# Weight sums split wholly on VectorE, their writes issued ahead of a step's loads, divisors sooner, key maxima one step later

## The chip, the cores and the metric

The kernel runs on one core of one Trainium2 chip. The metric is the device time of one execution in microseconds (us), as the median of several runs. TensorE (PE) multiplies matrices, VectorE (DVE), ScalarE (ACT) and GpSimd (POOL) do elementwise work, and SyncE (SP) issues every DMA of this kernel. Each engine works through its own list of instructions in order. Where an instruction waits, everything behind it on that engine waits too.

## The reference, cut to what matters

An attention over batch 4, heads 8, sequence 768, head dimension 64 is followed by a feed-forward part with 3072 tokens, 512 model columns and 2048 hidden columns:

```
k_sum = k.reshape(B, H, nb, block, D).max(axis=3)      # maxima of 32 keys
v_sum = v.reshape(B, H, nb, block, D).mean(axis=3)     # means of 32 values
scores_l = scale * q k^T, masked to |i - j| < 16;  scores_s = scale * q k_sum^T + log(block)
a = softmax of both side by side
attn_out = a @ [v, v_sum]
h = x @ w_in                      # x: attn_out as (3072, 512)
g = h * tanh(softplus(h))
out = g @ w_out
```

## The kernel before

**Tiles and steps.** The tokens are cut into 12 chunks of 256 and 6 groups of 512 (two chunks). The hidden columns are cut into 16 blocks of 128. A step is one (group, block): `ph` multiplies the group's x by a block of w_in (L501), `ff_act` applies the activation (L508), `ff_split` splits the result into a rounded upper part `ah` (ACT, L517) and the rest `al` (DVE, L519), and `ff_out` multiplies both by the block of w_out into `po` (L529). `ff_out` of step i-2 runs in step i. Groups 0 and 1 (steps 0 to 31) compute `ph` directly. From step 32 on, steps go in pairs: `ff_in_pair` computes the `ph` of two blocks with seven products of quarter blocks instead of eight (L738), as a Strassen-like scheme, and DVE puts them together (L748 to L756, tile `change`).

**Weight sums.** That scheme needs sums and differences of quarter blocks of w_in. They are made once, for eight pairs p of blocks, in two halves per pair: `first_sums` (L705, L706) and `second_sums` (L711, L712). `split_sums` rounds each into an upper part (L696, on ACT) and a rest (L697, on DVE). All of it lies in one scratch tile, `area` (in the profile: `results`). The halves are made in steps 19 to 30, one per step, and in steps 34, 36, 38 and 40. `keep` queues their writes to DRAM (`w_sums`, L689) in a list, `send` issues that list in the next step, and `load_sums` (L723) later reads a pair's sums into one of two buffers. A half overwrites the area that the half before is being written from, so its first DVE instructions wait until those writes have landed.

**Attention units.** One unit is one chunk and one pair of heads, 48 in all. From unit 18 on, units go two by two, at the steps in `begins`: 19, 22, 25, 29, 33, 37 and so on, every fourth step to 73. For a pair of units that begins at step i: `scores` (L345) with the maxima (L366) and exponents (L377, ACT) in step i, divisors (`rs`, L392 and L393, DVE) and normalisation (L397, POOL) in step i for the first unit and step i+1 for the second, transposes (`pt_ps`, L403, PE) in step i+2, values (`x_ps`, L429) where the next pair begins. `x_sum` (L457 to L463, DVE) turns the values into the x of a later group.

**Loads of a step.** `loads` issues, in this order: the queries and keys `qk` of the next two units (L304), what `keys` holds, the values `vw` (L321, L322), and what `sums` holds. `keys` of a unit copies its key maxima `km` into the `qk` tile (POOL, L309). For the first unit of a batch's head pair it first reduces the keys to `km` (DVE, L273) and then loads the values for their means, `vsum` (L239). `sums` of such a unit makes the means `vq` (DVE, L294, L295), writes them to a tile `vm` (L300) and loads the next head pair's keys `ks` (L235). `ks` and `vsum` share one buffer, so the four units of a batch form a chain: ks, km, vsum, vq, ks, km, and so on. Two such chains fall into the part that the change touches: units 24 to 27 (used by the scores of steps 29 and 33) and units 36 to 39 (scores of steps 53 and 57).

**What sets the order.** Up to step 18 the order is written out by hand and the diff does not touch it. From step 19 on it comes from two loops. A whole step (19 to 31) and the second step of a pair run `norms(i)`, `loads(i)`, `send()`, then queued x sums, `ff_out`, `turns`, and `weight_sums(i)` at the end. Between the first products of a pair and the next ones, `between` runs the exponents of a second unit. The steps at which a unit's `keys` and `sums` come are set by `put`:

```
put("keys", i + 2 * j, u + 2)
put("sums", min(i + 2 * j + 1, later - 1), u + 2)
```

Here j is 0 for the first and 1 for the second unit, and `later` is the step at which the next pair begins.

Of the kernel before, what the change touches and what calls it, by code (L numbers as in the profile page):

```python
# [10 lines left out]
F32R = mybir.dt.float32r  # L11
# [55 lines left out]
def fused_kernel(ctx: ExitStack, tc: tile.TileContext, q0, qk, kt, v0, vw, vs, w_in, w_out, out):  # L67
    nc = tc.nc
# [168 lines left out]
    def load_value_source(b, hp):  # L237
        vsum = sources[b, hp, 1] = stage.tile([VP, BLK, BLK], F32, tag="sum", name=f"vsum{b}_{hp}", bufs=1)
        nc.sync.dma_start(vsum, vs[b, hp].rearrange("p (d j) -> p d j", j=BLK))  # L239
# [71 lines left out]
    def att_load_keys(c, hp):  # L311
        b, th = divmod(c, CPB)
        if th == 0:
            key_summary(b, hp)
            load_value_source(b, hp)
        att_key_summary(c, hp)
# [8 lines left out]
    def att_summaries(u):  # L325

        for i, fs in ((u, (value_means, value_summary)), (u + 1, (load_key_source,))):
            if i < len(todo) and todo[i][0] % CPB == 0:
                for f in fs:
                    f(todo[i][0] // CPB, todo[i][1])  # L330
# [40 lines left out]
    def att_exponents(c, hp):  # L371

        u = units[c, hp]
        pr, nm = u["p"], u.pop("m")
        sm = small.tile([P, NQ], F32, tag="sm", name=f"sm{c}_{hp}")
        for s in range(NQ):
            nc.scalar.activation(pr[:, s, :], pr[:, s, :], AF.Exp, scale=-1.0, bias=nm[:, s:s + 1],  # L377
                                 accum_out=sm[:, s:s + 1])
        u["sm"] = sm
# [164 lines left out]
    steps = [(g, fc) for g in range(NG) for fc in range(NFC)]  # L544
# [135 lines left out]
    def send():  # L680
        while unsent:
            unsent.pop(0)()
# [10 lines left out]
            keep(p, part, 0, t[:, CH:3 * CH])  # L693

    def split_sums(p, first, whole, upper):
        nc.scalar.copy(upper.bitcast(F32R), whole)  # L696
        nc.vector.tensor_sub(whole.bitcast(F32R), whole, upper)  # L697
        keep(p, 0, first, upper)
        keep(p, 1, first, whole)
# [25 lines left out]
    def ff_in_pair(g, fc, pair, between):  # L725

        w = buffer(pair)
        banks = []

        def products(*found):  # L730
            ps = ps_w.tile([P, TG], F32, tag="w", name=f"ph{g}_{fc}_{len(banks)}")
            banks.append(ps)
            for half, m in enumerate(found):
                wh, wl = (w[:, part, (4, 3, 1, 2, 5, 6, 7).index(m), :] for part in range(2))
                xh, xl = x_piece(g, m)
                for a in range(2):
                    for n, (w_, x) in enumerate(((wh, xh), (wh, xl), (wl, xh))):
                        nc.tensor.matmul(turned(ps[:, half * CH:(half + 1) * CH]), w_[:, a * P:(a + 1) * P],  # L738
                                         turned(x[:, a, :]), start=(a == 0 and n == 0), stop=(a == 1 and n == 2))
            return ps  # L740

        first_, second = (ff.tile([P, TG], F32, tag="t", name=f"h{g}_{fc + k}", bufs=2) for k in range(2))
        low, high = slice(0, CH), slice(CH, TG)
        nc.scalar.copy(second, products(1, 3))
        between()
        ps = products(2, 6)
        nc.scalar.copy(first_[:, low], ps[:, low])  # L747
        nc.vector.tensor_sub(change, second[:, high], ps[:, low])  # L748
        nc.vector.tensor_add(change, second[:, low], change)
        nc.vector.tensor_add(first_[:, high], ps[:, high], change)  # L750
        ps = products(7, 5)
        nc.vector.tensor_add(second, ps, second)
        nc.vector.tensor_sub(second[:, low], second[:, low], ps[:, high])
        ps = products(4)
        nc.vector.tensor_add(first_[:, low], ps[:, low], first_[:, low])  # L755
        nc.vector.tensor_add(second[:, low], ps[:, low], second[:, low])  # L756
        st[g, fc], st[g, fc + 1] = first_, second

    at = {}

    def put(what, i, *found):
        at.setdefault((what, i), []).extend(found)
# [4 lines left out]
    for k, i in enumerate(begins):  # L767
        pair = [2 * n + 2 + 2 * k, 2 * n + 3 + 2 * k]
        later = begins[k + 1] if k + 1 < len(begins) else i + 4
        put("scores", i, *pair)  # L770
        put("turns", i + 2, *pair)
        put("values", later, *pair)
        for j, u in enumerate(pair):
            put("norms", i + j, u)
            put("keys", i + 2 * j, u + 2)
            put("sums", min(i + 2 * j + 1, later - 1), u + 2)

    def found(what, i):
        return [todo[u] for u in at.get((what, i), ()) if u < len(todo)]
# [1 line left out]
    def loads(i):  # L781
        for u in at.get(("scores", i), ()):
            if u + 2 < len(todo):
                att_queries(*todo[u + 2])
        for unit_ in found("keys", i):
            att_load_keys(*unit_)
        for u in at.get(("values", i), ()):
            if u + 2 < len(todo):
                att_load_values(*todo[u + 2])
        for u in at.get(("sums", i), ()):  # L790
            att_summaries(u)

    def norms(i):
        for unit_ in found("norms", i):
            att_divisors(*unit_)
            att_normalize(*unit_)
# [34 lines left out]
    for i in range(done, whole_steps):  # L831
        ff_in(*steps[i])
        ff_act(*steps[i])
        values(i)
        some = scores(i)
        lower = ff_split(*steps[i])
        for unit_ in some:
            att_exponents(*unit_)
        lower()
        norms(i)  # L840
        loads(i)
        send()
        for _ in waiting[:2 if some else 1]:
            waiting.pop(0)()
        ff_out(*steps[i - 2])
        turns(i)
        if whole_steps - i in (3, 2):
            load_sums(3 - (whole_steps - i))
        weight_sums(i)

    late_exponents = []
    for i in range(whole_steps, len(steps), 2):
        pair = (i - whole_steps) // 2
        ff_in_pair(*steps[i], pair, lambda: [att_exponents(*late_exponents.pop()) for _ in late_exponents[:]])
        ff_act(*steps[i])
        ff_act(*steps[i + 1])
        norms(i)
        ff_split(*steps[i])()
        while waiting:
            waiting.pop(0)()  # L860
        loads(i)
        send()
        ff_out(*steps[i - 2])
        weight_sums(i)
        load_sums(pair + 2)
        values(i + 1)
        some = scores(i + 1)
        if some:
            att_exponents(*some[0])
            late_exponents.extend(some[1:])  # L870
        ff_split(*steps[i + 1])()
        norms(i + 1)
        loads(i + 1)
        send()
        for _ in waiting[:2]:
            waiting.pop(0)()
        ff_out(*steps[i - 1])
        turns(i + 1)
        weight_sums(i + 1)
# [46 lines left out]
```

## Time and profile before

| | |
|---|---|
| median of 3 runs | 671.72 us (671.13 to 673.95) |
| the profiled execution | 673.55 us, of which the span in the trace is 671.6 us |
| PE busy in the span | 613.0 us (91%) |
| weight loads of PE (PEld) | 528.5 us (79%) |
| DVE | 427.8 us (64%) |
| ACT | 350.9 us (52%) |
| POOL | 82.5 us (12%) |
| DMA | 141.77 MB, mean 211 GB/s |

In the profile's picture of the span in 40 slices, PE is at 9 tenths or more almost everywhere. The exceptions are the beginning, one slice at 48% of the span, and slices 12 to 18 (about 185 to 302 us), where it falls to between 5 and 9 tenths. In the same slices the granted clock of TensorE falls below its full level. Lower down, the page lists groups of instructions and what ended the idle time before them. A wait is worth something only if PE waits for it in the end.

### The profile page before, as it was taken

What the parts mean: (1) busy time and instruction counts of PE and PEld (TensorE: products, weight loads), DVE (VectorE), ACT (ScalarE), POOL (GpSimd) and SP (SyncE); (2) the same over time, 40 slices, a digit from 0 to 9 for tenths busy, and PEclk for the clock granted to TensorE, in tenths of its full rate; (3) what the DMA queues carried; (4) which work ended last, traced back from release to release, by engine and by line L of the source; (5) the groups of instructions that cost most, each with busy time, mean ns of one, the idle gap of its engine ahead of it and who ended that gap; (6) DMA issues with size and microseconds to landing.
All of it is one profiled execution on the core that took longest, in us unless ns stands there. A gap on an engine that the chain in (4) does not pass through costs nothing.

```text
span 671.6 us, 12969 instructions
## 1 busy us (share of the span) xinstructions
PE 613.0 (91%) x4848; PEld 528.5 (79%) x4848; DVE 427.8 (64%) x1078; ACT 350.9 (52%) x827; POOL 82.5 (12%) x119
## 2 busy tenths in 40 slices
PE   4899999999979756479999999889999999999997
PEld 4787777788868545368889898778898988998996
DVE  5999999954655345366776676657675564744433
ACT  4985758764635224145656654535664654333232
POOL 4522122000120000001001101011100100000000
PEclk9999999999999787769999999999999999999999
DMA  9977766514475226659987867658867745365421
GB/s 281 284 231 257 256 210 225 201 47 136 147 236 185 96 71 198 246 180 338 331 302 242 271 231 255 237 190 311 288 210 243 251 147 213 128 264 197 141 101 63
DMA packets 50222, 141.77 MB, mean 211 GB/s; under 512 B 8816, under 2 KB 15728, under 8 KB 50160
## 3 DMA queue, kind: packets, MB, share of 16 engines
q1 hardware_dynamic: 50160, 140.94, 62.1%
q8 instruction: 39, 0.64, 0.4%
q14 instruction: 23, 0.19, 0.1%
HBM read 117.83 MB, written 20.97 MB: 207 GB/s over the span
## 4 chain that ended last, share of the span: by engine, by line
PE 54%; DMA 13%; DVE 12%; ACT 5%; SPq 3%; issue 2%; POOL 0%; DVEq 0%; POOLq 0%; ACTq 0%
PE po L529 25%; PE ph L738 18%; PE ph L501 5%; DMA vsum<-vs 3%; DMA w_sums<-results 3%; DMA qk<-qk 3%; PE x_ps L429 2%; PE sc L345 2%; DVE al L519 2%; DMA w_early_in<-w_sums 2%; DMA ks<-kt 2%; PE pt_ps L403 1%; DVE vq L294 1%; SPq L689 1%; DVE km L273 1%
## 5 line engine op out<-in xcount | busy, mean ns | idle before, releaser
L397 POOL TENSOR_TENSOR pr<-pr,rs 128x480 f32<-128x480 f32 x48 | 59.3, 1236 | 380.7 <-DVE rs L393 229.4
L738 PE MATMUL ph<-xh,w_early_in 128*128 128x256 f32 x512 | 100.1, 280 | 5.8 <-ACT a L508 5.8
L529 PE MATMUL po<-w_early_out_hi,al 128*128 128x512 f32 x240 | 93.5, 389 | 1.1 <-DVE al L519 1.1
L529 PE MATMUL po<-w_early_out_hi,ah 128*128 128x512 f32 x240 | 94.4, 393 | 0.0
L529 PE MATMUL po<-w_early_out_lo,ah 128*128 128x512 f32 x240 | 93.3, 389 | 0.0
L738 PEld LDWEIGHTS ph<-xh,w_early_in 128*128 128x128 f32 x512 | 83.7, 192 | 6.1 <-ACT a L508 6.1
L508 ACT ACTIVATE h<-h 128x512 f32<-128x512 f32 x64 | 36.9, 623 | 91.9 <-DVE h L755 91.9
L519 DVE TENSOR_TENSOR al<-h,ah 128x512 fp32r<-128x512 f32 x64 | 44.6, 713 | 56.0 <-ACT ah L517 56.0
L377 ACT ACTIVATE pr<-pr,nm 128x120 f32<-128x120 f32 x192 | 73.4, 385 | 11.5 <-DVE nm L366 11.2
L738 PE MATMUL ph<-xl,w_early_in 128*128 128x256 f32 x256 | 71.5, 279 | 0.0
L529 PE MATMUL po<-w_late_out_hi,ah 128*128 128x512 f32 x144 | 58.0, 403 | 0.0
L696 ACT CAST results<-results 128x512 fp32r<-128x512 f32 (+1 forms) x24 | 12.5, 546 | 84.5 <-DVE results L711 42.6
L529 PE MATMUL po<-w_late_out_lo,ah 128*128 128x512 f32 x144 | 56.4, 392 | 0.0
L529 PE MATMUL po<-w_late_out_hi,al 128*128 128x512 f32 x144 | 56.4, 392 | 0.0
L529 PEld LDWEIGHTS po<-w_early_out_hi,al 128*128 128x128 f32 x240 | 45.0, 188 | 10.4 <-DVE al L519 2.4
L501 PE MATMUL ph<-xh,w_early_in 128*128 128x512 f32 x160 | 53.1, 399 | 0.0
L529 PEld LDWEIGHTS po<-w_early_out_hi,ah 128*128 128x128 f32 x240 | 45.0, 188 | 9.5 <-issue 1.4
L529 PEld LDWEIGHTS po<-w_early_out_lo,ah 128*128 128x128 f32 x240 | 45.1, 188 | 9.2
L738 PEld LDWEIGHTS ph<-xl,w_early_in 128*128 128x128 f32 x256 | 49.1, 192 | 0.0
L403 PE MATMUL pt_ps<-ident,pr 128*120 128x128 f32 x192 | 28.5, 283 | 21.8 <-POOL pr L397 21.5
L748 DVE TENSOR_TENSOR change<-h,ph 128x256 f32<-128x256 f32 x32 | 13.4, 418 | 54.1 <-ACT h L747 54.0
L738 PE MATMUL ph<-w_late_in,w_early_in 128*128 128x256 f32 x320 | 47.6, 278 | 0.1
(110 smaller groups left out, 1252.6 us busy)
## 6 DMA issues: line engine op xcount, KB each, us to landing
w_early_in<-w_sums SPq DMA_DIRECT2D x64, 896.0 KB
qk<-qk SPq DMA_DIRECT2D x40, 496.0 KB
w<-w_in SPq DMA_DIRECT2D x16, 512.0 KB
w<-w_out SPq DMA_DIRECT2D x16, 512.0 KB
w_sums<-results SPq DMA_DIRECT2D x32, 256.0 KB
vw<-vw SPq DMA_DIRECT2D x40, 192.0 KB
ks<-kt SPq DMA_DIRECT2D x16, 384.0 KB
out<-results SPq DMA_DIRECT2D x24, 256.0 KB
```

Source lines behind the costliest of these rows:

```text
L345: nc.tensor.matmul(ps[h][row, at0:at0 + KA], u["qk"][r, s, h * QT:(h + 1) * QT], u["qk"][r, s, P:], start=True, stop=True)
L377: nc.scalar.activation(pr[:, s, :], pr[:, s, :], AF.Exp, scale=-1.0, bias=nm[:, s:s + 1], accum_out=sm[:, s:s + 1])
L397: nc.gpsimd.tensor_mul(u["p"], u["p"], u["r"].unsqueeze(2).broadcast_to([P, NQ, KA]))
L403: nc.tensor.transpose(ps[:KA, s * P:(s + 1) * P], u["p"][:, s, :], ident)
L429: nc.tensor.matmul(x, u["v"][0:rows, s, d], pt, start=(c >= CG), stop=(c >= CG or s == NQ - 1))
L501: nc.tensor.matmul(turned(ph), w[:, cc * P:(cc + 1) * P], turned(x[:, cc, :]), start=(cc == 0 and n == 0), stop=(cc == NCC - 1 and n == 2))
L508: nc.scalar.activation(a, st[g, fc], AF.Mish)
L519: return lambda: nc.vector.tensor_sub(al, a, ah.bitcast(F32))
L529: nc.tensor.matmul(turned(po[g][t]), a[:, tok], turned(w), start=(fc == 0 and n == 0), stop=(fc == NFC - 1 and n == 2))
L696: nc.scalar.copy(upper.bitcast(F32R), whole)
L738: nc.tensor.matmul(turned(ps[:, half * CH:(half + 1) * CH]), w_[:, a * P:(a + 1) * P], turned(x[:, a, :]), start=(a == 0 and n == 0), stop ...
L748: nc.vector.tensor_sub(change, second[:, high], ps[:, low])
```

## The change

Five edits, all of them from step 19 on:

- `split_sums` rounds the upper part on DVE (`tensor_copy`) and no longer on ACT.
- `send()` stands ahead of `loads(i)` in every step, so the writes of the last half of sums are issued ahead of the step's loads.
- In the pair steps, the divisors and the normalisation of a second unit move from after the activations into `between`, right behind the second unit's exponents.
- `keys` of a unit come one step later: i+1 for the first unit and, for the second, i+3 where the next pair begins at i+4 (i+2 where it begins at i+3). `sums` follow one step later too, at i+2 and at the latest in the step in which the next pair begins.
- In `loads`, `sums` come ahead of the values, since the means may now be written in the same step.

```diff
     def split_sums(p, first, whole, upper):
-        nc.scalar.copy(upper.bitcast(F32R), whole)
+        nc.vector.tensor_copy(upper.bitcast(F32R), whole)
         nc.vector.tensor_sub(whole.bitcast(F32R), whole, upper)
...
             put("norms", i + j, u)
-            put("keys", i + 2 * j, u + 2)
-            put("sums", min(i + 2 * j + 1, later - 1), u + 2)
+            put("keys", i + 1 + min(2 * j, later - i - 2), u + 2)
+            put("sums", min(i + 2 * j + 2, later), u + 2)
...
             att_load_keys(*unit_)
+        for u in at.get(("sums", i), ()):
+            att_summaries(u)
         for u in at.get(("values", i), ()):
             if u + 2 < len(todo):
                 att_load_values(*todo[u + 2])
-        for u in at.get(("sums", i), ()):
-            att_summaries(u)
...
         norms(i)
+        send()
         loads(i)
-        send()
...
+    def second_exponents(i):
+        while late_exponents:
+            att_exponents(*late_exponents.pop())
+        norms(i)
+
...
-        ff_in_pair(*steps[i], pair, lambda: [att_exponents(*late_exponents.pop()) for _ in late_exponents[:]])
+        ff_in_pair(*steps[i], pair, lambda: second_exponents(i))
         ff_act(*steps[i])
         ff_act(*steps[i + 1])
-        norms(i)
...
+        send()
         loads(i)
-        send()
```

**Where the instructions stand.** On SP, in steps 25 to 28, before. `w_sums_1966` and `w_sums_1965` are the DRAM tiles of two pairs, `ks`, `vsum` and `vm` belong to the chain of units 24 and 25:

```order
L235 DMA ks_0_2335<-kt 128x768
L689 DMA w_sums_1966<-w_early_in 128x512 x2
L689 DMA w_sums_1966<-results 128x512 x2
L304 DMA qk_0_2453<-qk 128x992
L304 DMA qk_1_2455<-qk 128x992
L239 DMA vsum_0_2459<-vs 96x1024
L321 DMA vw_2_2462<-vw 96x512
L322 DMA vw_2_2462<-vm_2_1579 24x4x128
L321 DMA vw_3_2465<-vw 96x512
L322 DMA vw_3_2465<-vm_3_1619 24x4x128
L689 DMA w_sums_1966<-results 128x512 x2
L689 DMA w_sums_1966<-results 128x256 x2
```

The same place now:

```order
L689 DMA w_sums_1966<-results 128x512 x4
L689 DMA w_sums_1966<-results 128x256 x2
L304 DMA qk_0_2455<-qk 128x992
L304 DMA qk_1_2457<-qk 128x992
L235 DMA ks_0_2459<-kt 128x768
L321 DMA vw_2_2461<-vw 96x512
L322 DMA vw_2_2461<-vm_2_1579 24x4x128
L321 DMA vw_3_2464<-vw 96x512
L322 DMA vw_3_2464<-vm_3_1619 24x4x128
L689 DMA w_sums_1965<-w_early_in 128x512 x2
L689 DMA w_sums_1965<-results 128x512 x2
L239 DMA vsum_0_2515<-vs 96x1024
```

The writes of a second half no longer stand behind the step's queries, the `vsum` load and the values, and the load of `vsum` stands behind the writes of the half that came before it.

On DVE, around steps 26 and 27, before (`al_10` and `al_11` belong to those steps, `rs_3` is a second unit's divisor):

```order
L519 TENSOR_TENSOR al_10_2507<-a_10_2504,ah_10_2506 128x512
L392 TENSOR_SCALAR rs_3_2510<-sm_3_2443 128x4
L393 RECIPROCAL rs_3_2510<-rs_3_2510 128x4
L294 TENSOR_REDUCE vq_0_2514<-vsum_0_2459 96x32
L295 TENSOR_SCALAR vq_0_2514<-vq_0_2514 96x32
L711 TENSOR_TENSOR results<-results 128x512
L712 TENSOR_TENSOR results<-results 128x256
L697 TENSOR_TENSOR results<-results 128x512
L697 TENSOR_TENSOR results<-results 128x256
```

Now:

```order
L519 TENSOR_TENSOR al_10_2502<-a_10_2499,ah_10_2501 128x512
L392 TENSOR_SCALAR rs_3_2505<-sm_3_2441 128x4
L393 RECIPROCAL rs_3_2505<-rs_3_2505 128x4
L273 TENSOR_REDUCE km_0_2513<-ks_0_2459 128x24
L711 TENSOR_TENSOR results<-results 128x512
L712 TENSOR_TENSOR results<-results 128x256
L696 CAST results<-results 128x512
L697 TENSOR_TENSOR results<-results 128x512
L696 CAST results<-results 128x256
L697 TENSOR_TENSOR results<-results 128x256
```

The casts stand on DVE, and the chain of keys and values is one step further back: `km` of unit 24 is now where `vq` of unit 24 was.

On DVE, just ahead of the maxima of step 57 (`km_3` is unit 39's, which the scores of step 57 use), before:

```order
L519 TENSOR_TENSOR al_8_4734<-h_8_4674,ah_8_4733 128x512
L294 TENSOR_REDUCE vq_3_4737<-vsum_3_4646 96x32
L295 TENSOR_SCALAR vq_3_4737<-vq_3_4737 96x32
L366 ISA pr_2_4792,nm_2_4793<-sc_2_0_4774,first 128x120
L366 ISA nm_2_4793 128x1
```

Now:

```order
L755 TENSOR_TENSOR h_8_4669<-ph_8_3_4717,h_8_4669 128x256
L756 TENSOR_TENSOR h_9_4670<-ph_8_3_4717,h_9_4670 128x256
L519 TENSOR_TENSOR al_8_4729<-h_8_4669,ah_8_4728 128x512
L273 TENSOR_REDUCE km_3_4732<-ks_3_4642 128x24
L366 ISA pr_2_4787,nm_2_4788<-sc_2_0_4769,first 128x120
```

The last maximum of keys that step 57 needs stood eight instructions and more ahead of this place, and now stands right in front of it.

## Rows read from the trace of the kernel before

**Rows 1.** Windows of the span: us, PE, PEld, DVE, ACT, POOL busy, clock, DMA share, GB/s.

```profile
230.00:255.00 25.00, 15.96 (x108) 12.08 (x106) 8.30 (x12) 4.75 (x9) 0.26 (x1) 0.83 0.38 129
255.00:280.00 25.00, 14.08 (x57) 11.49 (x58) 14.26 (x39) 9.95 (x26) 2.64 (x3) 0.79 0.59 204
```

**Rows 2.** Waits over the whole span: waiter, waited for, total us, times, longest.

```profile
PE pt_ps L403 <- POOL pr L397: 21.5, 7, 6.5
```

**Rows 3.** Timeline of SP's queue, steps 28 and 29: start, us, line, issues.

```profile
252.46 1.28 SPq L689 DMA_DIRECT2D w_sums<-results  x2
...
264.54 0.33 SPq L239 DMA_DIRECT2D vsum<-vs  x1
...
267.75 1.99 SPq L689 DMA_DIRECT2D w_sums<-results  x4
```

**Rows 4.** Timeline of DVE, steps 23 to 29: start, us, line, operation, idle before.

```profile
199.81 1.36 DVE L706 TENSOR_TENSOR results<-results 128x512 f32<-128x512 f32 x1
...
257.18 0.69 DVE L711 TENSOR_TENSOR results<-results 128x512 f32<-128x512 f32 x1 [7.17 <-DMA w_sums<-results]
...
263.59 0.92 DVE L273 TENSOR_REDUCE km<-ks 128x24 f32<-128x768 f32 x1
...
265.42 0.43 DVE L462 CAST w_early_in<-x_blocks 128x512 fp32r<-128x512 f32 x1
...
271.63 1.23 DVE L705 TENSOR_TENSOR results<-w_late_in 128x1024 f32<-128x1024 f32 x1 [3.99 <-DMA w_sums<-results]
272.89 0.69 DVE L706 TENSOR_TENSOR results<-results 128x512 f32<-128x512 f32 x1
```

**Rows 5.** Timeline of ACT in step 29: the cast and what its wait was.

```profile
257.91 0.92 ACT L696 CAST results<-results 128x512 fp32r<-128x512 f32 x2 [9.96 <-DVE results L711]
```

**Rows 6.** Timeline of PE in the same place.

```profile
259.38 0.79 PE L501 MATMUL ph<-xh,w_late_in 128*128 128x512 f32 x1 [5.75 <-ACT a L508]
```

**Rows 7.** The chain that ended last, PE's part: start, us, what.

```profile
166.13 2.72 PE ph L501 x12
...
177.02 0.87 PE pt_ps L403 x8
...
180.62 1.08 PE x_ps L429 x32
181.70 1.05 PE sc L345 x32
...
299.42 1.08 PE x_ps L429 x32
...
477.06 4.77 PE ph L738 x42
```

**Rows 8.** The same chain, steps 49 to 57: units 36 to 39.

```profile
401.79 0.84 DVE km L273
...
410.21 1.14 DVE vq L294
412.43 3.21 DMA ks<-kt
...
416.64 6.39 DMA vsum<-vs
...
425.43 4.29 DMA ks<-kt
...
430.73 8.97 DMA vsum<-vs
...
445.38 0.95 DVE km L273
448.78 1.04 PE sc L345 x30
```

**Rows 9.** Timeline of POOL, steps 24 and 53 to 55.

```profile
198.57 2.04 POOL L397 TENSOR_TENSOR pr<-pr,rs 128x480 f32<-128x480 f32 x1 [10.34 <-DVE rs L393]
...
436.74 0.26 POOL L309 COPY qk<-km 128x96 f32<-128x96 f32 x1 [7.67 <-DMA qk<-qk]
```

More of the change, by code (lines that the diff above doesn't have):

```diff
@@ L872, in fused_kernel @@
         norms(i + 1)
+        send()
         loads(i + 1)
-        send()
         for _ in waiting[:2]:
```

## Prediction

> **What bounds the kernel now.** I read the picture of the span in slices first: PE is the busiest engine, and from 320 us on it hardly stops, so work taken off another engine is worth nothing there. The windows show where it does stop [rows 1]: between 230 and 280 us PE is busy for 30.0 of 50 us, at a granted clock of 0.83 and 0.79, while DVE (22.6 us), ACT (14.7 us) and DMA (0.38 and 0.59) are far from full. So latency sets the time there, not work.
>
> The size of the loss: the value products of step 22 start at 180.62, those of step 33 at 299.42 [rows 7], 118.8 us. PE's own work between them at full clock is 9 `ph` of 2.72, 11 `po` (twelve products of the same size, so 2.72 each), one paired `ph` of 4.77, three turns of 0.87 and three times values and scores, 1.08 + 1.05 [rows 7]: 24.5 + 29.9 + 4.8 + 2.6 + 6.4 = 68.2 us. So **50.6 us** is the most that anything can win in these steps.
>
> What holds PE is a loop over four queues. SP issues the two writes of a first half at 252.46 [rows 3]. DVE's next half (L711) idles 7.17 us for their landing and starts at 257.18 [rows 4]. ACT's cast behind it had idled 9.96 us [rows 5], the activation stands behind the cast on ACT, and PE's next product idles 5.75 us for it [rows 6]. Then SP issues `vsum` only when `km` has ended on DVE (263.59 + 0.92 = 264.51, issue at 264.54), and the writes of the half made at 257 to 260 come behind that, at 267.75 [rows 3, 4]. So they lie for some 8 us although they are ready, and the next half starts at 271.63: one half every 14.45 us, where PE alone needs 68.2 / 11 = 6.2 us a step.
>
> **The casts.** A cast of this shape takes DVE 0.43 us [rows 4] against 0.46 on ACT (0.92 for two, rows 5). Sixteen of 128x512 and eight half as wide (estimated at 0.25) add 9 us to DVE, which idles 27 of the 50 us above, and take away the point at which ACT waits for DMA. A first half is then 1.23 + 0.69 + 0.43 + 0.69 = 3.0 us [rows 4], with a subtraction taken like L706; a second half about the same. What is queued behind DVE's wait for the writes is the next `al`; `ff_out` needs that two steps later, about 12 us, so a wait of a few us is covered.
>
> DVE and POOL disturb each other: L706 took 1.36 us instead of 0.69 while POOL's normalisation ran for 2.04 [rows 4, 9]. With a cast in that place I bound the loss at 0.7 us for each of the three turns in these steps, 0 to 2 us, and take 0, since a second unit's normalisation now has a whole step in hand.
>
> A rule of the Trainium skill speaks against the edit here ("SBUF — State Buffer", section "SBUF: two separate sides"): VectorE and GpSimd share one pair of SBUF ports, held for a whole instruction by the one that starts first, and an fp32 copy on VectorE takes it, while ScalarE has ports of its own. The slowed L706 agrees. By the rule the sum would be at most those 2 us longer.
>
> **The writes first.** Landing was seen at 257.18 - 253.74 = 3.4 us and 271.63 - 269.74 = 1.9 us after the last issue [rows 3, 4]. With one more issue of 0.5 us (1.99 for four) a half's loop becomes 3.0 + 0.5 + 1.9 to 3.4 = 5.4 to 6.9 us, say 6.2: PE's own pace. Steps 22 to 26 then run with PE full: step 26's `ph` ends at 180.62 plus 4 `ph`, 4 `po`, one turn and two times values and scores, 180.62 + 10.9 + 10.9 + 0.9 + 4.3 = 207.6.
>
> **Maxima and sums one step later.** Now the chain of units 24 to 27 limits. `km` of unit 24 comes in step 26, behind at most one loop of the halves: 207.6 + 6.2 = 213.8. A unit's round is `km` 0.95, issue 0.4, `vsum` 6.39 to 8.97, `vq` 1.14, 1.1 to the issue of `ks` (411.35 to 412.43), `ks` 3.21 to 4.29 [rows 8]: 13.2 to 16.9 us. Three rounds measured in steps 49 to 55 took 445.38 - 401.79 = 43.6, 14.5 each. In steps 26 to 32 the halves' writes and two loads of sums share the queue, and x sums stand between, so I take 16, with 13.2 and 19 as ends (19: the dearest round and 2 us of DVE work that the waits don't cover). Unit 27's `km` ends at 213.8 + 48 = 261.8, and the scores of step 33 follow it: its value products come at about 262 instead of 299.4. **Gain 37 us** (45 to 28).
>
> The other batch pays. Before, unit 36's `km` ran at 401.79 and its `vq`, one step later, at 410.21 [rows 8]; now `km` takes that place, and unit 39's `km` stands directly ahead of the scores of step 57. With the measured 43.6 us: 410.2 + 43.6 + 0.95 + 0.3 for POOL's copy [rows 9] = 455.1, where the scores of step 57 began at 448.78: 6.3 us. Each gap of PE was followed by a stretch at a lower clock [rows 1], for which I add 1.7. **Loss 8 us**; with rounds of 13.2 and 16.9 it is 1 to 14.5.
>
> **Divisors sooner.** POOL no longer holds a second unit's normalisation behind a copy that waits for `qk` (7.67 us at 436.74, rows 9). PE's waits for POOL, 21.5 us in all [rows 2], lie nearly all in the two stretches above and are in the gain already; elsewhere PE does not wait, so nothing.
>
> **Sum.** The profiled execution took 673.55 us (span 671.6). 673.55 - 37 + 8 = 644.5. It lies 1.8 us above the median of its three runs, so the median should come to **643 us**.
>
> **The rivals.** (1) *The rounds are dear.* `vsum` took 8.97 us behind other loads and 6.39 with fewer [rows 8]; now more is packed into less time. With 19 us and 16.9 us rounds: 673.55 - 28 + 14.5 - 1.8 = 658. For it: steps 22 to 33 move the same bytes in 81 us instead of 119. Against it: the DMA share was 0.38 and 0.59 [rows 1]. The Trainium skill ("DMA: Bandwidth & Descriptors", section "Queues, rings and completion order") says that each DMA engine takes the descriptors of a ring in order, so a load issued behind a large one starts after it. The 8.97 us agree, and by that rule this rival is the nearer one in steps 29 to 32.
>
> (2) *The chain hides.* With rounds of 13.2: 673.55 - 45 + 1 - 1.8 = 628. For it: the measured 6.39 held queueing too. Against it: three rounds measured 14.5 with no half being made.
>
> (3) *Slower.* The halves stay at over 13 us each because the landing of the writes sets them, wherever they stand on SP; DVE then waits with `al` queued behind it as ACT waited, nothing is won, and the late maxima of steps 52 and 56 cost their 8 to 14.5 us: 680 to 686. It decides from the point at which a half's loop in steps 25 to 30 stays above 13 us. Against it: landings of 1.9 and 3.4 us [rows 3, 4].
>
> (4) *Nothing changes.* SP stands in front of the writes at another wait, such as `qk` for PE's scores, as long as before: 669 to 675. Against it: the scores come ahead of the half in every step.
>
> **How the numbers follow.** Forecast 0.62, rival (1) 0.18, (2) 0.12, (3) 0.05, (4) 0.03. The range has to reach to (1) and (2): 624 to 661. About 0.5% (3.4 us) is what a measurement here can tell from no change. Faster by more: 0.92; within: 0.03, rival (4); slower: 0.05, rival (3).
>
> **What would show it.** Right: ACT has no idle time before a cast of sums; DVE's halves in steps 22 to 29 start 6 to 9 us apart; the value products of step 33 start at 255 to 270 us; PE waits at the scores of steps 53 and 57 for POOL's copy, that is for `km`. Wrong: halves still 13 us apart (rival 3 or 4); no PE wait at 53 and 57 (rival 2); `vsum` taking 9 us and more in steps 26 to 32 (rival 1). The prediction fails outright if DVE, now behind the writes, makes PE wait for `al`.

## The result, and the profile after

The median fell from 672.84 us (671.13 to 676.32, 4 runs) to **642.42 us** (641.8 to 643.63, 4 runs): a ratio of 0.954 with a 95% interval of 0.950 to 0.959. The profiled execution after took 642.63 us, its span is 640.9 us against 671.6 before. The forecast was 643 us in a range of 624 to 661.

Three windows of the span (columns as in [rows 1]):

```profile
205.00:230.00 25.00, 25.00 (x170) 20.70 (x169) 19.98 (x40) 11.89 (x29) 2.71 (x4) 1.00 0.76 247
230.00:255.00 25.00, 18.52 (x85) 15.55 (x83) 17.88 (x47) 8.97 (x25) 2.64 (x3) 0.86 0.94 316
255.00:280.00 25.00, 23.04 (x182) 20.21 (x183) 17.41 (x49) 12.87 (x32) 2.80 (x5) 0.93 0.62 217
```

PE is now full at a granted clock of 1.00 (2.4 GHz) until the window that begins at 230 us. In that one it still stops, but DMA stands at 0.94 of its 16 engines where it stood at 0.38 [rows 1]. So the place of the loss is the same and its nature is another.

What PE waits for after, over the whole span (us, times, longest):

```profile
...
PE sc L345 <- POOL qk L309: 4.6, 2, 2.8
PE ph L738 <- DMA w_early_in<-w_sums: 4.5, 2, 2.8
PE ph L738 <- DVE w_early_in L462: 3.7, 1, 3.7
PE pt_ps L403 <- POOL pr L397: 2.3, 2, 1.4
...
PE ph L738 <- DVE nm L366: 1.2, 1, 1.2
```

(The row left out at the top is the wait for the first queries, 8.6 us, which the change does not touch.) The 21.5 us of [rows 2] are 2.3. New are the loads of sums, an x sum (L462), and POOL's copy of the maxima at the scores of steps 53 and 57.

The halves of the sums on DVE in steps 28 to 30, and what SP issued for them (columns as in [rows 3, 4]):

```profile
227.62 0.69 DVE L711 TENSOR_TENSOR results<-results 128x512 f32<-128x512 f32 x1 [1.73 <-DMA w_sums<-results]
...
237.09 1.22 DVE L705 TENSOR_TENSOR results<-w_late_in 128x1024 f32<-128x1024 f32 x1
...
250.62 0.69 DVE L711 TENSOR_TENSOR results<-results 128x512 f32<-128x512 f32 x1 [6.61 <-DMA w_sums<-results]
...
256.06 0.43 DVE L462 CAST w_early_in<-x_blocks 128x512 fp32r<-128x512 f32 x1
...
263.85 0.95 DVE L273 TENSOR_REDUCE km<-ks 128x24 f32<-128x768 f32 x1
```

```profile
229.13 2.04 SPq L689 DMA_DIRECT2D w_sums<-results  x4
...
238.61 0.99 SPq L723 DMA_DIRECT2D w_early_in<-w_sums  x2
...
240.91 1.17 SPq L689 DMA_DIRECT2D w_sums<-results  x2
```

The writes of the half of 227.62 go out at 229.13, while it is being made; before, they lay for 8 us. Up to step 29 the halves start 5 to 10 us apart. The last one breaks the row: the writes that it waits for stand behind a load of sums (L723) and land 8.5 us after the end of their issue (242.08), DVE waits 6.61 us, the x sum of 256.06 waits behind it, and PE behind that:

```profile
247.92 2.50 PE L738 MATMUL ph<-w_early_in 128*128 128x256 f32 x10 [2.79 <-DMA w_early_in<-w_sums]
256.64 0.35 PE L738 MATMUL ph<-w_early_in 128*128 128x256 f32 x1 [3.65 <-DVE w_early_in L462]
```

The stretches between value products (`x_ps`, L429, from first product to first product), in us, for the profiled execution of each kernel, the experiments too:

| kernel | steps 22 to 33 | 33 to 49 | 49 to 61 | median us | ratio to before (95%) |
|---|---|---|---|---|---|
| before | 118.8 | 96.2 | 76.5 | 672.84 | 1 |
| after | 81.9 | 97.4 | 79.0 | 642.42 | 0.954 (0.950 to 0.959) |
| e1 casts alone | 112.8 | 94.5 | 75.0 | 666.70 | 0.985 (0.982 to 0.989) |
| e2 writes first alone | 86.4 | 96.5 | 75.5 | 641.61 | 0.947 (0.943 to 0.951) |
| e3 casts and writes first | 81.2 | 94.7 | 75.5 | 634.76 | 0.938 (0.935 to 0.942) |
| e4 after, keys and sums early | 78.8 | 95.2 | 77.0 | 638.50 | 0.943 (0.939 to 0.947) |
| e5 after, casts on ACT | 84.5 | 100.4 | 77.1 | 648.76 | 0.960 (0.952 to 0.967) |
| e6 after, divisors late | 82.1 | 98.3 | 75.7 | 639.20 | 0.944 (0.939 to 0.950) |
| e7 after, loads of sums sooner | 88.0 | 97.0 | 77.7 | 647.73 | 0.957 (0.951 to 0.963) |
| e8 after, one half in step 32 | 80.1 | 101.2 | 79.1 | 646.07 | 0.955 (0.949 to 0.962) |
| e9 after, writes ahead of loads | 85.1 | 97.9 | 77.1 | 644.59 | 0.954 (0.951 to 0.957) |
| e10 e3 with e9's order | 80.6 | 94.4 | 75.2 | 634.34 | 0.940 (0.937 to 0.943) |
| e11 e10, copies apart | 80.0 | 94.7 | 76.3 | 634.52 | 0.939 (0.937 to 0.942) |
| e12 e10 without two loads | 75.5 | 94.8 | 75.9 | 629.68 | 0.933 (0.928 to 0.937) |

The runs came in several groups, each with its own runs of before (medians of 672.84 to 677.29 us), so the ratios are what compares across groups: e1 to e4 are one group, e5 to e8 another, e9 to e11 a third, and e12 stands alone. A stretch is read from one execution, and that lies up to 2.6 us from the median of its kernel (e4: 635.89 us), so differences of one or two us between stretches are rough.

### The profile page after: what moved, and what is told of

The parts are those of the page before. It is cut to its first block, busy times and chain, and to the rows that moved or that the text cites. A ratio compares the mean times of both kernels' runs of the same rounds, so it can differ in the third digit from the quotient of the medians.

```text
span 640.9 us, 13019 instructions
## 1 busy us (share of the span) xinstructions
PE 606.7 (95%) x4848; PEld 524.3 (82%) x4848; DVE 439.2 (69%) x1102; ACT 339.9 (53%) x803; POOL 80.1 (12%) x119
## 4 chain that ended last, share of the span: by engine, by line
PE 56%; DVE 18%; DMA 6%; ACT 6%; issue 3%; POOL 0%; DVEq 0%; POOLq 0%; ACTq 0%; SPq 0%
PE po L529 27%; PE ph L738 17%; PE ph L501 7%; DMA w_sums<-results 4%; PE x_ps L429 2%; DVE al L519 2%; ACT pr L377 2%; PE sc L345 1%; PE pt_ps L403 1%; DMA vsum<-vs 1%; DVE vq L294 1%; DVE w L173 1%; ACT ah L517 1%; ACT L377 1%; DVE change L749 1%
## 5 line engine op out<-in xcount | busy, mean ns | idle before, releaser
L397 POOL TENSOR_TENSOR pr<-pr,rs 128x480 f32<-128x480 f32 x48 | 57.7, 1204 | 337.9 <-DVE rs L393 166.2
L529 PE MATMUL po<-w_early_out_hi,ah 128*128 128x512 f32 x240 | 95.8, 399 | 0.0
L529 PE MATMUL po<-w_early_out_hi,al 128*128 128x512 f32 x240 | 94.7, 394 | 0.7 <-DVE al L519 0.6
L529 PE MATMUL po<-w_early_out_lo,ah 128*128 128x512 f32 x240 | 94.8, 395 | 0.0
L519 DVE TENSOR_TENSOR al<-h,ah 128x512 fp32r<-128x512 f32 x64 | 43.2, 691 | 57.5 <-ACT ah L517 57.5
L738 PE MATMUL ph<-w_early_in 128*128 128x256 f32 x256 | 41.3, 288 | 9.7 <-DMA w_early_in<-w_sums 4.5
L744 ACT COPY h<-ph 128x512 f32<-128x512 f32 x32 | 18.8, 586 | 56.7 <-PE ph L738 56.7
```

Source lines behind the costliest of these rows:

```text
L397: nc.gpsimd.tensor_mul(u["p"], u["p"], u["r"].unsqueeze(2).broadcast_to([P, NQ, KA]))
L519: return lambda: nc.vector.tensor_sub(al, a, ah.bitcast(F32))
L529: nc.tensor.matmul(turned(po[g][t]), a[:, tok], turned(w), start=(fc == 0 and n == 0), stop=(fc == NFC - 1 and n == 2))
```

## The experiments

**Which edits carry the gain (e1 to e3).**

```diff
-        nc.scalar.copy(upper.bitcast(F32R), whole)
+        nc.vector.tensor_copy(upper.bitcast(F32R), whole)
```

> The kernel before with one edit: the casts of the weights' sums on VectorE. Theory (a loop over SP's order and ScalarE's cast, of which the writes' place on SP is the larger part): the writes still stand behind the step's loads, so the halves stay about 13 us apart and DVE still waits 4 to 8 us for their landing; only ACT's wait goes, and PE may run up to two steps ahead. 655 to 668 us, that is 4 to 17 us faster than before, with the value products of step 33 at 282 to 296 us. Rival (ACT's wait is the whole of it, since only it reaches PE): 640 to 650 us. Rival (late key maxima carry the gain): no change, 669 to 674 us.

Measured: 666.7 us, as expected (value products of step 33 at 297.1 us, a little later than expected). DVE still waited 47.8 us for the writes (41.3 before), and that wait now reached PE through `al`, which the prediction had called covered:

```profile
DVE results L711 <- DMA w_sums<-results: 29.0, 7, 7.3
DVE results L705 <- DMA w_sums<-results: 18.8, 5, 6.1
```

```profile
262.50 0.79 PE L529 MATMUL po<-w_late_out_hi,al 128*128 128x512 f32 x1 [7.87 <-DVE al L519]
```

So while the writes stand behind the loads, the cast's engine mainly decides by what route the wait gets to PE; it is worth 1.5%. For e2, in all three places:

```diff
-        loads(i)
         send()
+        loads(i)
```

> The kernel before with one edit: the writes of a half are issued ahead of the step's loads; casts stay on ScalarE. Theory (the place on SP is the larger part of the loop): the halves come 6 to 9 us apart, ACT's idle time before a cast of sums falls from 10 us to below 4, and 645 to 655 us follow, the value products of step 33 at 270 to 282 us. Rival (ACT's wait is the whole of it): 660 us or more. Rival (late key maxima carry the gain): 669 to 674 us.

Measured: 641.61 us, a larger gain than expected. This edit alone takes 32.4 of the 37 us in steps 22 to 33. ACT still waits for the halves, up to 8.4 us where below 4 was expected, but PE hardly feels it: its waits for `a`, the activation behind such a cast, fall from 19.3 us to 3.1 (from 180 us on):

```profile
ACT results L696 <- DVE results L706: 29.5, 8, 5.4
ACT results L696 <- DVE results L711: 21.8, 8, 8.4
```

For e3, both edits:

> The kernel before with two edits, casts on VectorE and writes first; keys, sums and divisors stay where they were. Theory: these two make the whole gain of steps 22 to 33, and without late keys steps 49 to 61 lose nothing: 637 to 642 us, value products of step 33 at 255 to 264 us, no wait of PE for POOL's copy at the scores of steps 53 and 57. Rival (the chain of keys and values limits steps 26 to 33, and its new place carries part of the gain): 646 us or more.

Measured: 634.76 us, better than expected, 6.9 us below e2 and 3.7 below the changed kernel with its early divisors and old maxima (e4). These two edits are the whole gain of steps 22 to 33 (37.6 us). And although keys and sums are a step earlier here, the value products of step 33 start at 263.64 us; in the changed kernel it is 263.56. So the chain of keys and values did not set that time. In e3 unit 27's maximum ends 9 us ahead of those value products; what both kernels share is DVE's wait for writes behind a load of sums (6.61 us above), with an x sum behind it:

```profile
250.34 0.69 DVE L711 TENSOR_TENSOR results<-results 128x512 f32<-128x512 f32 x1 [5.65 <-DMA w_sums<-results]
...
253.74 0.95 DVE L273 TENSOR_REDUCE km<-ks 128x24 f32<-128x768 f32 x1
```

**What the other edits cost (e4 to e6).** For e4:

```diff
-            put("keys", i + 1 + min(2 * j, later - i - 2), u + 2)
-            put("sums", min(i + 2 * j + 2, later), u + 2)
+            put("keys", i + 2 * j, u + 2)
+            put("sums", min(i + 2 * j + 1, later - 1), u + 2)
```

> The changed kernel with keys and sums put back to their old steps; casts, writes and divisors as changed. Theory: late keys only cost here, by the 4.6 us for which PE waits for POOL's copy at the scores of steps 53 and 57 of the changed kernel: 637 to 641 us. Rival (late keys are part of the gain, since vsum no longer stands ahead of other work): 645 us or more. Rival (they change nothing): 641.5 to 643.5 us.

Measured: 638.5 us, as expected. With keys and sums at their old steps, sums never fall into a step with values, so the fifth edit (sums ahead of values) changes nothing here: SP's, ACT's and POOL's instructions are those of e3, and e4 differs from e3 by the early divisors. What late keys cost includes the fifth edit, which was not tried apart from them. For e6:

```diff
             att_exponents(*late_exponents.pop())
-        norms(i)
...
         ff_act(*steps[i + 1])
+        norms(i)
```

> The changed kernel with the divisors and the normalisation of second units back behind the activations of the pair steps. Theory: nothing hangs on them, 641.5 to 644 us. Rival (they are what keeps PE from waiting for POOL's normalisation in the pair steps, now that a copy which waits for late maxima can stand ahead of it): 645 to 650 us.

Measured: 639.2 us, below what was expected: neither theory had a gain there. In per cent of the time before, late maxima with early divisors cost 1.1 over e4, early divisors with late maxima 1.0 over e6; e3, with neither, stands 0.5 below e4 with all of its runs below all of e4's. The intervals of e3 and e4 overlap, as do those of e6 and the changed kernel by a hair, and e6 is from another group, so the shares are rough. That late maxima cost rather than win is clear: the intervals of e4 and the changed kernel do not meet. For the divisors it rests on both comparisons and on the rounds below.

What the divisors cost is seen in one group of DVE's list (L749, the second of the pair's seven additions; busy, mean ns), first after, then e6:

```profile
L749 DVE TENSOR_TENSOR change<-h,change 128x256 f32<-128x256 f32 x32 | 21.0, 656 | 1.1
```

```profile
L749 DVE TENSOR_TENSOR change<-h,change 128x256 f32<-128x256 f32 x32 | 13.6, 425 | 1.1
```

And in one place of step 46, after, on DVE and on POOL:

```profile
346.34 0.18 DVE L393 RECIPROCAL rs<-rs 128x4 f32<-128x4 f32 x1
346.43 0.39 DVE L748 TENSOR_TENSOR change<-h,ph 128x256 f32<-128x256 f32 x1
346.86 1.09 DVE L749 TENSOR_TENSOR change<-h,change 128x256 f32<-128x256 f32 x1
```

```profile
346.69 0.99 POOL L397 TENSOR_TENSOR pr<-pr,rs 128x480 f32<-128x480 f32 x1 [2.53 <-DVE rs L393]
```

The early divisor releases POOL's normalisation just ahead of L749, which then takes 1.09 us instead of 0.42. The same holds in all eleven rounds with a second unit: 1.09 or 1.10 us there, 0.42 or 0.43 in the other 21 instructions of the group. With 0.3 us for the divisor itself, DVE's additions end 1 us later, the last x sum (L463) with them, and the round from step 45 to 49 takes 24.5 us where e3 takes 23.7. So it is in every kernel: that round and the one from step 61 take 24.5 us each in the six with early divisors (after, e4, e5, e7, e8, e9) and 23.7 in the eight without. This is the disturbance that the prediction bounded at 0 to 2 us and looked for at the casts only; the rule it quoted from the Trainium skill ("SBUF — State Buffer", section "SBUF: two separate sides") agrees with the 1.09 us: POOL's instruction starts first, ends at 347.68, and L749 ends 0.27 us later.

For e5, the first diff undone:

> The changed kernel with the casts of the sums back on ScalarE. Theory (writes first is the larger part, the cast a smaller one): ACT waits again for DVE's half, some 2 to 4 us in each of the steps that are tight, and PE behind it: 645 to 652 us. Rival (with short landings the cast's engine doesn't matter): 641 to 644 us. Rival (the cast is the larger part): 655 us or more.

Measured: 648.76 us, as expected; the cast on DVE is worth 0.5% of the time before in the changed kernel, with intervals that overlap, and 6.9 us where the other edits are left out (e3 against e2).

**What limits steps 29 to 33 now (e7 to e12).** The theory was the loads of sums and what is queued behind them.

```diff
-    ... enumerate((4, 4, 3, 3, 2, 2, 1, 1, 0, 0, 5, 5))}
+    ... enumerate((0, 0, 1, 1, 2, 2, 3, 3, 4, 4, 5, 5))}
...
-        if whole_steps - i in (3, 2):
-            load_sums(3 - (whole_steps - i))
+        if whole_steps - i in (5, 3):
+            load_sums((5 - (whole_steps - i)) // 2)
```

> The changed kernel with the halves made in the order of pairs 0, 1, 2, 3, 4, 5 (it was 4, 3, 2, 1, 0, 5), which frees the first buffer two steps sooner, and the two loads of sums issued in steps 27 and 29 instead of 29 and 30. Theory (from step 29 on the changed kernel is held by the loads of sums and by the writes queued behind them, not by the chain of keys and values): PE's waits of 4.5 us for the loads go, DVE's wait of 6.6 us before the half of step 30 falls below 3, the x sums behind it come sooner, and the value products of step 33 start at 251 to 258 us instead of 263.6: 631 to 637 us. Rival (the chain limits there): value products of step 33 at 262 us or later, 640 to 644 us. Rival (bytes through the DMA engines limit, whatever the order): 640 to 646 us.

Measured: 647.73 us, value products of step 33 at 268.8 us: the expectation fell. PE's wait for the loads is gone, but DVE now waits behind each of the two loads:

```profile
232.58 0.69 DVE L711 TENSOR_TENSOR results<-results 128x512 f32<-128x512 f32 x1 [7.73 <-DMA w_sums<-results]
...
255.05 0.69 DVE L711 TENSOR_TENSOR results<-results 128x512 f32<-128x512 f32 x1 [6.09 <-DMA w_sums<-results]
```

```profile
221.24 0.90 SPq L723 DMA_DIRECT2D w_early_in<-w_sums  x2
...
223.19 1.09 SPq L689 DMA_DIRECT2D w_sums<-results  x2
```

Writes issued at 223.19, 2 us behind a load of 1.8 MB, let the next half start only at 232.58. Landing was 1.9 to 3.4 us where no load stood ahead [rows 3, 4].

For e8:

```diff
-    ... enumerate((4, 4, 3, 3, 2, 2, 1, 1, 0, 0, 5, 5))}
+    ... enumerate((4, 4, 3, 3, 2, 2, 1, 1, 0, 0, 5))}
+    order_of_sums[whole_steps] = (5, 1)
```

> The changed kernel with one half, the second of pair 5, made in step 32 instead of step 30; the loads of sums stay. Theory (loads and the half behind them hold PE from step 29 on): the x sums of step 32 no longer stand behind DVE's wait of 6.6 us, so PE's wait of 3.7 us for them goes, while its 4.5 us for the loads stay: 638 to 641 us, value products of step 33 at 259 to 261 us. Rival (the chain limits): 642 to 644 us, since the maximum of unit 27 comes no sooner.

Measured: 646.07 us, the same ratio as the changed kernel, and not what was expected. PE's wait for the x sum fell only from 3.65 to 2.56 us, since DVE now waited 7.3 us for `vsum` ahead of it. Steps 22 to 33 took 1.8 us less, and the half in step 32 gave it back: it uses the tile that the stores of group 1 use in step 33, and PE then waited for ACT's copy into it (L539):

```profile
276.21 0.80 PE L529 MATMUL po<-w_early_out_hi,ah 128*128 128x512 f32 x1 [3.69 <-ACT results L539]
```

For e9, halves and loads as in e7, and in the two steps with a load:

```diff
+        weight_sums(i)
         if whole_steps - i in (5, 3):
+            send()
             load_sums((5 - (whole_steps - i)) // 2)
-        weight_sums(i)
```

> The changed kernel with the halves in the order of pairs 0 to 5 and the loads of sums in steps 27 and 29, as in the run before it, but in these two steps the half is made first, its writes are issued at once, and the load of sums behind them. Theory (a half's writes that are issued right behind a load of sums land only after that load, 8 us later, and everything queued on VectorE behind the next half waits with it): no half waits more than 3 us for its writes, PE waits neither for the loads nor for an x sum by more than 1 us each, the value products of step 33 start at 252 to 258 us: 632 to 638 us. Rival (the chain of keys and values is the limit): value products of step 33 at 262 us or later, 641 us or more. Rival (the bytes themselves are the limit, in whatever order): 641 us or more, with the same waits spread elsewhere.

Measured: 644.59 us, value products of step 33 at 266.4 us. The waits for the writes are gone as forecast, and the time isn't. On DVE, in place of them:

```profile
238.56 1.22 DVE L294 TENSOR_REDUCE vq<-vsum 96x32 f32<-96x1024 f32 x1 [4.34 <-DMA vsum<-vs]
...
256.26 1.22 DVE L294 TENSOR_REDUCE vq<-vsum 96x32 f32<-96x1024 f32 x1 [3.20 <-DMA vsum<-vs]
```

Now `vsum` stands behind the load of sums, and PE waits 5.61 us for a normalisation and 4.86 us for the x sum that stand behind these waits. For e10 the same order was put into e3:

> The kernel before with casts on VectorE and writes first (keys, sums and divisors as before), and the same new order of halves, writes and loads of sums. Theory: the 8 to 11 us between steps 29 and 33 go as in the run with late keys, and steps 37 to 61 keep what late keys and early divisors cost: 624 to 630 us, value products of step 33 at 252 to 257 us. Rival (chain or bytes): 633 to 636 us.

Measured: 634.34 us, no gain over e3, as the rival had it, value products of step 33 at 262.4 us. Its chain of waits shows `ks` at twice its usual time, where [rows 8] had 3.21 and 4.29:

```profile
228.03 6.88 DMA ks<-kt
...
244.86 7.13 DMA ks<-kt
...
373.62 3.22 DMA ks<-kt
```

Its DMA share in the window from 230 to 255 us is 0.97, at 333 GB/s:

```profile
230.00:255.00 25.00, 17.03 (x88) 13.93 (x87) 19.60 (x50) 9.01 (x25) 3.33 (x4) 0.91 0.97 333
```

Four orders of the same transfers (after, e7, e9, e10) gave value products of step 33 at 262 to 269 us. PE's last wait ahead of them is for the same x sum (L462) in all four, 3.65, 7.79, 4.86 and 6.15 us. What changes is the transfer that DVE waits for ahead of that sum: writes (after, e7), `vsum` (e9), `ks` (e10). The DMA share does not go with the time: e7, the latest, has 0.83 in this window, and e3 has 1.00. The last run takes the bytes away: the first two loads of sums, 3.7 MB, are left out of e10.

```diff
-        if pair < (NG - WHOLE) * NFC // 2:
+        if 2 <= pair < (NG - WHOLE) * NFC // 2:
```

> The kernel with casts on VectorE, writes first and the new order of halves and loads, without the first two loads of sums (pairs 0 and 1 of the first paired group, 3.7 MB; the products then multiply with what lies in the buffers). Everything else stays. Theory (from step 28 to 32 the bytes through the DMA engines set the time: at a DMA share of 0.9 to 1.0 in 230 to 255 us each order of the same transfers gave value products of step 33 at 261 to 269 us, and only the wait that shows it changed): the loads of keys take 3 to 4.5 us instead of 6.9 and 7.1, PE hardly stops, the value products of step 33 start at 250 to 255 us, 622 to 628 us. Rival (the chain of keys and values, with its latencies and its places on VectorE, limits whatever else is loaded): value products of step 33 at 259 us or later, 631 us or more.

Measured: 629.68 us, value products of step 33 at 257.7 us, between the two expectations. Of the 12.4 us by which e10 exceeds PE's own 68.2 us in these steps, 5.1 go with the two loads. Leaving them out takes away their bytes and their place ahead of other transfers at once, so the run does not tell the two apart, and the intervals of its ratio and e10's just overlap. Of the other 7.3, more than half is one wait of PE, for the same x sum. Window 230 to 255 us of e12, and that wait:

```profile
230.00:255.00 25.00, 20.59 (x107) 17.82 (x106) 21.87 (x54) 9.11 (x26) 2.74 (x4) 0.93 0.73 223
```

```profile
250.63 0.36 PE L738 MATMUL ph<-w_early_in 128*128 128x256 f32 x1 [3.79 <-DVE w_early_in L462]
```

DVE is busy for 21.9 of 25 us, and the x sum comes when DVE gets to it, not when a transfer ends: VectorE's work, or the order of it, looks like the next bound. An x sum placed ahead of the half and of the chain's instructions on DVE is the obvious rival, and it was not tried; nor was it tried apart that the casts, 0.42 us each, now lie on the path there.

**POOL's copy apart from the maximum (e11).**

```diff
             put("keys", i + 2 * j, u + 2)
+            put("copies", i + 1 + min(2 * j, later - i - 2), u + 2)
```

(`keys` then makes the maximum and loads `vsum`, `copies` only L309.)

> The run before it with one more edit: the maximum of keys and the load of values stay at their early step, and only POOL's copy of the maximum into the tile of the scores goes one step later, behind the normalisation of the second unit. Theory (early maxima cost nothing, and the copy that stands ahead of a normalisation makes PE wait for it, 2.8 us at step 55 with a stretch at a lower clock): the round from step 53 to 57 falls from 28.2 to 24 to 25 us, no wait of PE for POOL over 1 us from step 33 on: 2 to 4 us faster than the run before it. Rival (qk, not the place of the copy, is late there): no change.

Measured: 634.52 us, no change. PE's wait for the normalisation in step 55 fell from 2.23 us (e10) to 0.27, and in step 57 PE waited 2.47 + 0.55 us for DVE's `h`, against 0.71 in e10. Behind it:

```profile
405.64 0.95 DVE L273 TENSOR_REDUCE km<-ks 128x24 f32<-128x768 f32 x1 [3.46 <-DMA ks<-kt]
```

The maximum waits for its load with the pair's additions queued behind it. This wait stands in e10 too (3.40 us), and PE, which came 2 us later there, did not feel it.

## Why the prediction was right, and where it was not

**The gain, 37 us: measured 36.9, by another last step, so the size was met by luck.** The loop was as described: with the writes first the halves come 5 to 10 us apart (6.2 forecast, 6.8 on average in steps 22 to 29), ACT has no cast to wait for, and PE is full from step 22 to about 243 us. The step that failed is "now the chain of units 24 to 27 limits". Its maxima stand at 213.1, 224.9, 241.0 and 263.9 us, and 261.8 was forecast for the end of the last, but that one did not wait for its keys: their last packet had ended at 259.2, and DVE reached it without idle time (263.85 above), after an x sum that PE was waiting for. With the chain a step earlier (e3) the time was the same. What holds PE is that x sum on DVE, behind transfers that queue up behind loads of sums; how much of it is bytes (at most 5.1 us by e12), how much order on the queue and on DVE, stays open. Rival (1) had loads behind loads, though not their price. Its sign, `vsum` of 9 us and more, came once: by the trace's packets the three loads of steps 26 to 30 took 3.0, 3.2 and 9.1 us, the last one behind a load of sums (issued at 242.17, ended at 251.31), and DVE did not wait for it.

The prediction gave the casts no part of their own. In these steps they are worth 6.0 us alone and 5.2 beside the writes; the writes alone are worth 32.4.

**The loss, 8 us: measured 2.5 in steps 49 to 61.** The kind was right, POOL's copy makes PE wait at the scores of steps 53 and 57:

```profile
389.06 0.64 PE L345 MATMUL sc<-qk 64*64 64x120 f32 x16 [2.81 <-POOL qk L309]
...
416.26 0.64 PE L345 MATMUL sc<-qk 64*64 64x120 f32 x16 [1.81 <-POOL qk L309]
```

The term was mis-sized in its rounds: 14.5 us each was taken from [rows 8], and the chain after, in steps 49 to 57, shows 11.2, 16.6 and 11.1, 38.9 us in place of 43.6. In the third round `vsum` now stood ahead of a load of sums (issued at 404.78, the load at 405.21) and no longer behind one (430.73 and 425.99 before). It took 3.58 us there in place of 8.97, and 3.54 in the first round:

```profile
376.02 0.96 DVE km L273
376.99 3.54 DMA vsum<-vs
```

(The ends that the prediction gave for this term, 1 and 14.5, come out of its own rows as 4.0 and 15.1.) And a wait of PE in these steps before, for a normalisation behind such a copy, is gone; the prediction held these waits to be in the gain already and took nothing off the loss. Before, 400 to 460 us (slices 26 and 27 of the page, the only ones between the first stretch and the end in which PE falls below 9 tenths; there is none at 48%):

```profile
PE pt_ps L403 <- POOL pr L397: 3.6, 1, 3.6
```

So the waits nearly balance, and the loss shows in PE's busy time. The rounds from step 53 and from step 57, before and then after:

```profile
419.11:446.53 27.42, 23.79 (x206) 21.12 (x205) 14.78 (x43) 13.31 (x33) 2.47 (x3) 1.00 0.66 216
446.53:472.01 25.48, 24.24 (x205) 21.33 (x204) 17.78 (x50) 14.91 (x36) 3.03 (x5) 1.00 0.80 280
```

```profile
384.52:412.73 28.21, 25.40 (x205) 22.28 (x204) 17.94 (x49) 13.66 (x34) 2.74 (x4) 0.94 0.71 248
412.73:439.94 27.21, 25.40 (x205) 22.27 (x204) 15.39 (x45) 14.65 (x36) 2.85 (x5) 0.94 0.66 229
```

PE is busy for 50.8 us in place of 48.0, and idle for 4.6 in place of 4.9. Behind each of the two waits the granted clock fell to 0.50 (1.2 GHz), as in the window from 417.4 to 420.7 us. The round from step 57 in e6, where PE waited 1.00 us instead of 1.81:

```profile
413.52:438.32 24.80, 23.80 (x206) 21.14 (x205) 14.85 (x44) 13.96 (x35) 3.09 (x5) 1.00 0.72 246
```

There the clock stayed at 1.00 and the same work took PE 23.80 us instead of 25.40. That is 1.6 us, where 1.7 had been added; but it came twice, and the prediction had counted it once. Its reason, that each gap of PE was followed by a lower clock, does not hold for every gap: before, the wait of 3.6 us above left the clock at 1.00 throughout the round.

**Divisors sooner, nothing: this failed.** The prediction looked at what POOL no longer holds up, and not at what now runs beside POOL. It costs some 3 to 7 us (3.7 for e4 against e3, 1.0% for after against e6), of which the traces show 1.6, 0.8 in each of the rounds from step 45 and from step 61; where the rest lies was not found.

**The sum.** 36.9 gained, 1.2 lost in steps 33 to 49, 2.5 in 49 to 61, 0.8 in 61 to 69 and 0.5 behind them, and all of it begins 1.1 us later, at a wait for the first queries that the change does not touch (the kernels of the table differ by up to 3.8 us there). That leaves 30.8 us; the spans differ by 30.7. So 643 was met with a gain of the right size for another reason, a loss put 5.5 us too high, and some 4 us of losses that it did not have. That these nearly cancel is luck. The sign that it had named for its failure, PE waiting for `al`, was hardly seen after (0.6 us in all, 1.1 before), but in e1 (11.4 us).

**What was left on the table.** e3, two of the five edits, takes 634.76 us: 1.6% of the time before below the changed kernel by ratio, with intervals that do not meet. e10 and e11 are level with it, and none was faster with all of the work in it.

## What to carry to other kernels

Where a buffer is filled again only after its last contents have been written out, issue those writes ahead of every transfer that nobody waits for yet; look both at what stands ahead of them on the issuing engine and at what stands ahead of them in the DMA queue. When several orders of the same work each bring up a new wait at the same time, look for the instruction that the busiest engine waits for in all of them and for what stands ahead of it in its queue, and count bytes and busy time in that window, before trying another order. Undo the edits of a change one by one even when the whole is faster: here two of five were the gain, and two others took a quarter of it back.

## What the runs showed of the hardware that had not been expected

The writes of a half (512 or 768 KB in pieces of 128 and 256 KB) landed 1.9 to 3.4 us after their last issue with no load of sums ahead of them [rows 3, 4], and 7.9 to 8.5 us after when they stood behind a load of 1.8 MB issued some 2 us earlier (8.5 in the changed kernel, 8.3 and 7.9 in e7), read from when DVE's next half could start. `ks` behaves the same way: in e10 6.88 and 7.13 us behind such a load, 3.05 to 3.22 later in the same run. So does `vsum` in the changed kernel: 9.1 us against 3.0 and 3.2. The Trainium skill ("DMA: Bandwidth & Descriptors", section "Queues, rings and completion order") says that a ring's descriptors are taken in order by each DMA engine, and all of these agree.

An addition of 128x256 on DVE took 1.09 us instead of 0.42 when POOL's multiplication of 128x480 started just ahead of it, while POOL's took 0.99 us. In these eleven places the loss is DVE's alone. It is not always so: in [rows 4, 9] both were slow, 1.36 us on DVE and 2.04 on POOL.
